# Chunked state recurrence and two feed-forward layers on one core: direct scores for eight tiles, causality by a product, weights decoded in the prologue, mixing by a shifted column, weights on 64-byte lines

## The chip, the core and the metric

The kernel runs on one core of a Trainium2 chip. The metric is device time in microseconds (us) for one execution; lower is better. The engines are TensorE (PE in the profile; PEld is its weight load), VectorE (DVE), ScalarE (ACT), GpSimd (POOL) and SyncE (SP), which here only issues transfers. TensorE's products read SBUF and write PSUM.

## The reference, cut to what matters

```python
def _attn_ref(x, a, B, C):                       # batch 4, heads 8, S 768, D 32, N 16, chunk 32
    cum = np.cumsum(la, axis=-1)
    L = np.exp(cum[:, :, :, None] - cum[:, :, None, :]) * causal
    M = np.einsum('bhin,bhjn->bhij', Cc, Bc) * L
    y_intra = np.einsum('bhij,bhjd->bhid', M, xc)
    y_inter = np.einsum('bhin,bhnd->bhid', Cc, state) * np.exp(cum)[:, :, :, None]
    state = decay_full * state + sum_j(Bc x xc * decay_from_j)
...
def _moe_ref(x, mu_k, mu_r, w_k, w_v, w_r):      # batch 4, S 768, d 256, d_ff 1024
    xk = mu_k * x + (1.0 - mu_k) * x_prev        # x_prev: the token before, 0 at a batch's start
    xr = mu_r * x + (1.0 - mu_r) * x_prev
    k = np.maximum(xk @ w_k, 0.0)
    v = k * k @ w_v
    return sigmoid(xr @ w_r) * v
...
def _moe2_ref(x, w_in, w_out):                   # 3072 tokens, d 256, d_ff 2048
    h = x @ w_in
    return (h - np.tanh(h)) @ w_out
```

## The kernel before

The recurrence is computed in 24 tiles of 128 tokens (six in each of four batches). For a tile, `decays` multiplies prepared rows into differences of summed logarithms (`pd`), ScalarE takes their exponential into `L`, GpSimd's `causal` clears what lies in the future, `scores` makes C times B for 8 heads (`pcb`), VectorE's `mask` multiplies the two in place, and `outputs` multiplies `L` with x and adds the carried state (`py`); `next_state` and `tile_out` write the state and the result `xall` (256 channels on 2 x 128 partitions, tokens along the free dimension).

`scores` has two forms. Tiles 0 to 3 are direct: B as it lies in memory (16 states of 8 heads on 128 partitions) is the stationary operand, and the moving one is `cm`, C spread to one block of columns for each head with zeros elsewhere, which `head_columns` builds on VectorE and GpSimd; both are plain float32. Tiles 4 to 23 take B and C in high and low parts from `st`: `bc_load` loads, `bc_high` (ScalarE) and `bc_low` (VectorE) split, `bc_write` stores them to memory, and `bc_read` loads them in another order, for two tiles at a time.

The first feed-forward layer works on six blocks of 512 tokens. `shift` takes the difference of a block with itself one token later, `mix` makes xk and xr from it, `high` and `low` split them for exact products; `up`, `relu`, `square`, `high`, `low`, `down_part` follow four times per block, and `receptance` and `sigmoid` give the gate. The second layer has six blocks of eight units (`up2`, a polynomial for the tanh, `down2`): 12 products of 512 columns up and 12 down in each. All of its products are three for one (high x high, low x high, high x low).

Weights are decoded on the chip: `decode` fetches a chunk of 8-byte numbers (`raw`, two buffers), squares a part on ScalarE, and takes `top`, `sign`, `bottom`, `guard` on VectorE, `high` on either and `low` on VectorE. The first layer has nine such chunks, the second sixteen; the second layer's live where the recurrence's tiles lay, and are decoded when these are done with.

The order is written in two ways. START lists the prologue by hand: the setup of the decay rows, tiles 0 and 1 and their loads. Everything after it is tasks that `Plan.run` places one by one on the engines by its own costs, with ranks (RANK_T, RANK_F and the like) to choose between ready ones; what comes out is a fixed order for each engine. Where such an order puts an instruction behind one that waits, it waits too.

In each partition the first layer's weights begin at a multiple of 64 bytes, and the second layer's, which are laid out from the memory's other end, 32 bytes past one.

Of the kernel before, what the change touches and what calls it, by code (L numbers as in the profile page):

```python
# [9 lines left out]
F32R = mybir.dt.float32r  # L10
U32 = mybir.dt.uint32
# [5 lines left out]
P = 128  # L17
# [7 lines left out]
BLK = 512  # L25
# [3 lines left out]
NP2 = DFF2 // (2 * P)  # L29
NU2 = NBLK * NP2  # L30
# [4 lines left out]
RANK_F0, RANK_F, RANK_R, RANK_U, RANK_D = 30.0, 27.0, 9.0, 5.5, 16.1  # L35
RANK_G0, RANK_G, RANK_LAG = 173.3, 1.4, 9.7
RANK_W0, RANK_W = 0, 5.5
RANK_X0, RANK_X = 105.0, 5.2
# [12 lines left out]
    Da Dc neg idle za kr1 kr0 cA seg Dla Db lA hA Da2 hm cC warm Dca rA cB rh lB rl Db2 cD g2 lC zb Dx lD kr2 g1 Dc2 Dc1 W  # L51
    hB Dnr g0 tri Dx2 rB las d0 r2 bd p00 d1 heads dec p01 Dnk m0 p10 p11 w1 w0 m1 ps g4 o0 nu W gs cum o1 g3 k1 z1
# [130 lines left out]
def chain_kernel(ctx, tc, xb, a, an, a0, bt, bc, mu_k, mu_r, w_k, w_v, w_r, w_in, w_out, out):  # L183
# [25 lines left out]
    def vec(tag, dtype=F32, n=BLK):  # L209
# [3 lines left out]
    nuk = const.tile([P, 2], F32, name="nuk")  # L213
    nur = const.tile([P, 2], F32, name="nur")
# [3 lines left out]
    carry = const.tile([P, 2, NBLK], F32, name="carry")  # L218
    sums = const.tile([P, NU2 + 1], F32, name="sums")
    ones = const.tile([P, 1], F32, name="ones")  # L220
    okc = const.tile([P, 1], F32, name="okc")
# [4 lines left out]
    xall = zp.tile([P, 2, NTOK], F32, name="xall")  # L226
# [12 lines left out]
        pair=Ring(3), xb=Ring(2, 0, 1), bc=Ring(3, 0, 1, 2), hl=Ring(1), st=Ring(2, "c0", "c1"), L=Ring(2, 0, 1), bp=Ring(3, 0, 1), cp=Ring(2, 0),  # L239
        er=Ring(1, 0), erl=Ring(2, 0), state=Ring(2, 0, 1), raw=Ring(2, 0, 1), x=Ring(WORK["xh"], "b0"), l=Ring(WORK["l"], "p0"), h=Ring(WORK["h"], "p0", "p1"),  # L240
        s=Ring(WORK["s"], "p0"), acc=Ring(1), ob=Ring(3), raw2=Ring(2), f=Ring(WORK["f"], "p0", "p1"), wd=Ring(1), keep=Ring(2), wd2=Ring(1), keep2=Ring(2),
# [17 lines left out]
    def decode(n, job, pool, two, rank, after=(), fetched=False):  # L259

        N, ring = 2 * CW, R["raw" + two]
        raw = None if fetched else add(dict(S=0.42), lambda e: fetch(job()[0], n, pool()), after, rank, [(ring, n)], dma=1.35)
        use = [(ring, n)]

        def square(e):
# [3 lines left out]
        def top(e):  # L269
# [15 lines left out]
        def low(e):
# [3 lines left out]
        sq = add(dict(A=t_act(N)), square, [raw], rank, [keep], use)  # L289
        t1 = add(dict(V=t_dve2(N)), top, [raw], rank, [wd], use, port=True)  # L290
        t2 = add(dict(V=t_dve(N)), sign, [t1], rank, uses=use, port=True)
        t3 = add(dict(V=t_dve(N)), bottom, [t2], rank, uses=use, port=True)
        t4 = add(dict(V=t_dve(N)), guard, [t3, sq], rank, (), [wd, keep], port=True)
        t5 = add(dict(A=t_act(N), V=t_dve2(N)), high, [t4], rank, (), [keep], port=True)
        t6 = add(dict(V=t_dve(N)), low, [t5], rank, (), [keep], port=True)
        return t6, t6
# [41 lines left out]
    def bc_load(k):  # L338
        nc.sync.dma_start(out=bc_tile(k), in_=bc[:, :, k * GT:(k + 1) * GT])
# [726 lines left out]
```

## Time and profile before

| | |
|---|---|
| time, median of 3 runs | 542.42 us (541.08 to 545.35) |
| the profiled execution's own time | 544.08 us |
| its span, first to last instruction | 542.4 us |
| PE busy | 506.3 us, 93% |
| DVE busy | 425.1 us, 78% |
| ACT busy | 311.0 us, 57% |
| POOL busy | 43.4 us, 8% |
| mean granted TensorE clock | 0.954 |

A busy share is an average over stages with different limits: the recurrence's first tiles, a stretch in which tiles and the first layer alternate, the rest of the first layer beside the decoding of the second's weights, and the second layer by itself. A matmul's end is modelled and matmuls overlap, so the beat of a dense stretch is read from the starts of its rows.

### The profile page before, as it was taken

To read this page: it belongs to the slowest core of one execution; us is meant where nothing else is said; L and a number is where in the kernel's file an instruction comes from. 1 tells how busy PE (TensorE), PEld (TensorE's weight loads), DVE (VectorE), ACT (ScalarE), POOL (GpSimd) and SP (SyncE) were. 2 spreads that over 40 slices of the span, in tenths; PEclk is the share of its full clock that TensorE was granted. 3 is DMA by queue.
4 is the path that set the end of the run, shared out by engine and by line. 5 is a ranking of instruction groups with operands and counts; after the bars stand their busy time and mean duration, and the time that the engine had idled before them with its cause. 6 is when DMAs were issued, how large, how long until landed. Compare 5 with 4: busy or idle time off the path is not lost.

```text
span 542.4 us, 7272 instructions
## 1 busy us (share of the span) xinstructions
PE 506.3 (93%) x2754; PEld 384.8 (71%) x2754; DVE 425.1 (78%) x548; ACT 311.0 (57%) x394; POOL 43.4 (8%) x49
## 2 busy tenths in 40 slices
PE   5857779999999999999999999999999999999994
PEld 2424457777677778878768878887887887888783
DVE  8779889886875989999999977756867667775671
ACT  3334356567575567766665566456665566546650
POOL 8312100111211200000000000000000000000000
PEclk9775589999999999999999999999999999999999
DMA  4489996978765033232300000001001001000101
GB/s 130 136 217 244 227 253 158 195 180 174 151 118 99 1 118 116 79 95 102 114 1 1 0 17 24 1 0 40 0 1 40 0 2 39 1 0 1 39 2 44
DMA packets 27015, 42.82 MB, mean 79 GB/s; under 512 B 2766, under 2 KB 16390, under 8 KB 26974
## 3 DMA queue, kind: packets, MB, share of 16 engines
q1 hardware_dynamic: 26974, 42.29, 31.0%
q8 instruction: 24, 0.39, 0.3%
q14 instruction: 17, 0.14, 0.1%
HBM read 33.67 MB, written 8.59 MB: 78 GB/s over the span
## 4 chain that ended last, share of the span: by engine, by line
PE 76%; DVE 12%; DMA 7%; issue 2%; ACT 2%; SPq 1%; POOL 0%; POOLq 0%; ACTq 0%; DVEq 0%
PE acc L743 11%; PE acc L745 11%; PE acc L744 11%; PE ph L733 8%; PE ph L736 8%; PE ph L734 8%; PE pk L733 4%; PE pk L734 3%; PE pk L736 3%; PE py L492 2%; DMA st<-dbc 2%; PE pd L407 2%; PE pcb L457 2%; DMA raw<-in_w_k 1%; DVE wd L274 1%
## 5 line engine op out<-in xcount | busy, mean ns | idle before, releaser
L874 DVE SCALAR_TENSOR_TENSOR f<-f,s 128x1024 f32<-128x1024 f32 (+1 forms) x49 | 58.9, 1202 | 64.9 <-ACT f L870 64.3
L869 ACT ACTIVATE s<-ph 128x1024 f32<-128x1024 f32 (+1 forms) x49 | 49.3, 1006 | 88.7 <-PE ph L736 88.1
L745 PE MATMUL acc<-l,wouth 128*128 128x512 f32 x192 | 76.0, 396 | 1.1 <-DVE l L887 1.1
L743 PE MATMUL acc<-h,wouth 128*128 128x512 f32 x192 | 76.3, 397 | 0.8 <-DVE flag L945 0.8
L733 PE MATMUL ph<-xh,winh 128*128 128x512 f32 x192 | 76.0, 396 | 0.0
L744 PE MATMUL acc<-h,woutl 128*128 128x512 f32 x192 | 75.8, 395 | 0.0
L734 PE MATMUL ph<-xh,winl 128*128 128x512 f32 x192 | 75.7, 394 | 0.0
L300 ACT ACTIVATE h<-f 128x1024 fp32r<-128x1024 f32 (+1 forms) x54 | 56.3, 1043 | 15.1 <-PE acc L744 8.0
L878 DVE TENSOR_TENSOR f<-ph,f 128x1024 f32<-128x1024 f32 (+1 forms) x49 | 58.8, 1200 | 3.5
L736 PE MATMUL ph<-xl,winh 128*128 128x512 f32 x192 | 60.4, 395 | 0.0
L887 DVE TENSOR_TENSOR l<-f,h 128x1024 fp32r<-128x1024 f32 (+1 forms) x49 | 58.5, 1195 | 0.5
L870 ACT ACTIVATE f<-s,pbias 128x1024 f32<-128x1024 f32 (+1 forms) x49 | 55.6, 1135 | 1.6
L743 PEld LDWEIGHTS acc<-h,wouth 128*128 128x128 f32 x192 | 36.0, 187 | 10.8 <-ACT ob L300 1.1
L745 PEld LDWEIGHTS acc<-l,wouth 128*128 128x128 f32 x192 | 36.0, 187 | 10.6 <-DVE l L887 1.9
L306 POOL TENSOR_SCALAR_AFFINE_SELECT L<-L 128x1024 f32<-128x1024 f32 (+1 forms) x26 | 31.2, 1204 | 142.7 <-ACT L L412 133.2
L736 PEld LDWEIGHTS ph<-xl,winh 128*128 128x128 f32 x192 | 35.9, 187 | 9.1 <-DVE xl L857 0.4
L733 PEld LDWEIGHTS ph<-xh,winh 128*128 128x128 f32 x192 | 36.0, 187 | 8.9
L734 PEld LDWEIGHTS ph<-xh,winl 128*128 128x128 f32 x192 | 36.0, 187 | 8.7
L744 PEld LDWEIGHTS acc<-h,woutl 128*128 128x128 f32 x192 | 36.0, 188 | 8.5
L733 PE MATMUL pk<-xh,wkh 128*128 128x512 f32 x96 | 40.6, 422 | 0.0
L734 PE MATMUL pk<-xh,wkl 128*128 128x512 f32 x96 | 39.0, 406 | 0.0
L743 PE MATMUL acc<-h,wvh 128*128 128x512 f32 x96 | 38.3, 399 | 0.1
(142 smaller groups left out, 848.0 us busy)
## 6 DMA issues: line engine op xcount, KB each, us to landing
dbc<-hl SPq DMA_DIRECT2D x20, 256.0 KB
st<-dbc SPq DMA_DIRECT2D x20, 256.0 KB
st<-dbc SPq DMA_DIRECT2D x40, 128.0 KB
xbt<-in_xb SPq DMA_DIRECT2D x12, 384.0 KB
bct<-in_bc SPq DMA_DIRECT2D x11, 384.0 KB
raw<-in_w_in SPq DMA_DIRECT2D x8, 512.0 KB
raw<-in_w_out SPq DMA_DIRECT2D x8, 512.0 KB
out<-ob SPq DMA_DIRECT2D x12, 256.0 KB
```

Source lines behind the costliest of these rows:

```text
L300: A.activation(out=out, in_=in_, func=AF.Copy)
L733: PE.matmul(o, wh[:, k, ms], hi[:, k], start=k == 0, stop=False)
L734: PE.matmul(o, wl[:, k, ms], hi[:, k], start=False, stop=False)
L736: PE.matmul(o, wh[:, k, ms], lo[:, k], start=False, stop=k == 1)
L743: PE.matmul(acc[:, c], wh[:, k, cs], h[:, e], start=first, stop=False, skip_group_check=True)
L744: PE.matmul(acc[:, c], wl[:, k, cs], h[:, e], start=False, stop=False, skip_group_check=True)
L745: PE.matmul(acc[:, c], wh[:, k, cs], l[:, e], start=False, stop=last, skip_group_check=True)
L869: A.activation(out=s, in_=phs[j, i][:, e], func=AF.Square, accum_out=sums[:, c:c + 1])
L870: A.activation(out=qs[j, i][:, e], in_=s, func=AF.Square, scale=PA, bias=pbias)
L874: V.scalar_tensor_tensor(out=q, in0=q, scalar=PG, in1=s, op0=ALU.add, op1=ALU.mult)
L878: V.tensor_tensor(out=q, in0=phs[j, i][:, e], in1=q, op=ALU.mult)
L887: V.tensor_tensor(out=l[:, e], in0=qs[j, i][:, e], in1=f(h[:, e]), op=ALU.subtract)
```

## The change

Eight tiles in place of four are direct. C is laid out with its zeros on the host (`c4`, one 128 x 512 block of float32 per tile) and loaded; `head_columns` goes. The blocks are arranged so that the two halves of a tile use 64 partitions each. The split, store and reload are left out for those eight tiles, of whose `bc` only the third part is loaded. In those tiles causality is no longer cleared by GpSimd: a second product adds -32768 above the diagonal to `pd` before the exponential. The rows of `kr` for the first batch come from `kl` instead of the copy in memory. The prologue decodes the first two weight chunks step by step, the order of the nine chunks is another, and the three `kr` copies move to ScalarE. `xall` gets a zero column ahead of each batch, so that the previous token is the column before: `shift` and its carried columns go, `mix` becomes a scaled copy on ScalarE and one operation on VectorE (`mix_ahead`). One 32-byte tile (`okc`) moves into the second layer's pool, which puts that layer's weights at multiples of 64 bytes. Some ranks change.

```diff
+ND = 8
+NW = 2
...
-RANK_F0, RANK_F, RANK_R, RANK_U, RANK_D = 30.0, 27.0, 9.0, 5.5, 16.1
-RANK_G0, RANK_G, RANK_LAG = 173.3, 1.4, 9.7
-RANK_W0, RANK_W = 0, 5.5
-RANK_X0, RANK_X = 105.0, 5.2
+RANK_F0, RANK_F, RANK_R, RANK_U, RANK_D = 30.0, 27.0, 9.0, 5.5, 16.07
+RANK_G0, RANK_G, RANK_LAG = 144.89, 0, 6.52
+RANK_W0, RANK_W = 1.49, 5.5
+RANK_X0, RANK_X = 105.0, 6.14
...
-    xall = zp.tile([P, 2, NTOK], F32, name="xall")
+    xall = zp.tile([P, 2, NTOK + 8], F32, name="xall")
...
     def bc_load(k):
-        nc.sync.dma_start(out=bc_tile(k), in_=bc[:, :, k * GT:(k + 1) * GT])
+        w = slice(0, 3) if 2 * k >= ND else slice(2, 3)
+        nc.sync.dma_start(out=bc_tile(k)[:, w], in_=bc[:, w, k * GT:(k + 1) * GT])
...
     def rows(i):
...
+        if b:
+            nc.sync.dma_start(out=f(krs[i % 3][ONE:ONE + 2]), in_=dcum[:, b, :, ts])
+            return
+        for x, o in enumerate((CH, CL)):
+            nc.sync.dma_start(out=f(krs[i % 3][ONE + x:ONE + x + 1]), in_=f(kls[0][o:o + NH, ts]))
...
-            PE.matmul(pd[:, g], kls[b % 2][:, t * P:(t + 1) * P], krs[i % 3][:, 4 * g:4 * g + 4], start=True, stop=True)
+            PE.matmul(pd[:, g], kls[b % 2][:, t * P:(t + 1) * P], krs[i % 3][:, 4 * g:4 * g + 4], start=True, stop=i >= ND)
+            if i < ND:
+
+                PE.matmul(pd[:, g], ident, after.unsqueeze(1).to_broadcast([P, NH // 2, P]), start=False, stop=True)
...
-            if split:
-                causal(i, g)
...
-    def direct(i, pcb, g):
-        PE.matmul(pcb[:, 2 * g:2 * g + 2], bs[0][:, i * P:(i + 1) * P], cm[i][:, 4 * g:4 * g + 4], start=True, stop=True)
+    def c4_load(lo, hi):
+        o = cms[lo // NQ].rearrange("p a q s -> p (a q s)").rearrange("p (t c) -> p t c", c=BLK)
+        nc.sync.dma_start(out=o[:, lo % NQ:lo % NQ + hi - lo], in_=c4[lo:hi].rearrange("t p c -> p t c"))
+
+    def direct(i, pcb):
+        for g in range(2):
+            r = slice(64 * g, 64 * g + 64)
+            PE.matmul(pcb[:, g], bs[0][r, i * P:(i + 1) * P], cm[i][r], start=True, stop=True)
...
-            return lambda: V.tensor_copy(krs[i], neg.unsqueeze(2).to_broadcast([NR, NH, P]))
+            return lambda: A.activation(out=krs[i], in_=neg.unsqueeze(2).to_broadcast([NR, NH, P]), func=AF.Copy)
...
-            SEL[i] = put(dict(G=1.17), lambda e, i=i: causal(i), [E[i]], at(i) - 0.9, (), [(R["L"], i)])
+            SEL[i] = E[i] if i < ND else put(dict(G=1.17), lambda e, i=i: causal(i), [E[i]], at(i) - 0.9, (), [(R["L"], i)])
...
-    def shift(j):
...
-        V.tensor_tensor(out=u[:, :, 1:], in0=xall[:, :, t0 + 1:t1], in1=xall[:, :, t0:t1 - 1], op=ALU.subtract)
...
     def mix(nm, j):
         full = mixes[nm, j] = vec("f")
-        nu = nuk if nm == "k" else nur
+        x, o = block(j, 1), halves(full)
         for c in range(2):
-            V.scalar_tensor_tensor(out=full[:, c], in0=us[j][:, c], scalar=nu[:, c:c + 1], in1=xall[:, c, j * BLK:(j + 1) * BLK], op0=ALU.mult, op1=ALU.add)
+            A.activation(out=o[:, c], in_=x[:, c], func=AF.Copy, scale=mus[nm][:, c:c + 1])
+
+    def mix_ahead(nm, j):
+        x, o = block(j, 0), halves(mixes[nm, j])
+        for c in range(2):
+            V.scalar_tensor_tensor(out=o[:, c], in0=x[:, c], scalar=oms[nm][:, c:c + 1], in1=o[:, c], op0=ALU.mult, op1=ALU.add)
...
-        jobs1 = [jk[0], jr[0], jk[1], jk[2], jv[0], jk[3], jv[1], jv[2], jv[3]]
+        jobs1 = [jk[0], jk[1], jv[0], jk[2], jr[0], jv[1], jk[3], jv[2], jv[3]]
...
+            w2["okc"] = w2p.tile([P, 1], F32, name="okc")
             w2["ob"] = w2p
```

On VectorE, before, this is what stood between the mask of tile 1 and the mask of tile 2 (`L<-pcb,L` is a mask, `wd` and `keep` belong to a weight chunk, `bp` to `weigh`, `hl` to `bc_low`, `cm` is C spread by head); the rows shown begin at the last spreading of C.

```order
L435 TENSOR_TENSOR cm<-bct,hm 128x1024
L271 TENSOR_SCALAR wd<-raw 128x512
L422 TENSOR_TENSOR bp<-xbt,dec 128x128
L274 SCALAR_TENSOR_TENSOR wd<-raw,wd 128x512
L347 TENSOR_TENSOR hl<-bct,hl 128x2x256
L277 SCALAR_TENSOR_TENSOR wd<-raw,wd 128x512
L422 TENSOR_TENSOR bp<-xbt,dec 128x128
L280 SCALAR_TENSOR_TENSOR keep<-keep,wd 128x512
L422 TENSOR_TENSOR bp<-xbt,dec 128x128
L271 TENSOR_SCALAR wd<-raw 128x512
```

The first chunk's decoding began only after tile 1 and the spreading of C, with the split of B and C in its midst.

The same place on VectorE now, up to the masks of tiles 2 and 3.

```order
L640 TENSOR_SCALAR omr<-mur 128x2
L289 SCALAR_TENSOR_TENSOR wd<-raw,wd 128x512
L292 SCALAR_TENSOR_TENSOR wd<-raw,wd 128x512
L295 SCALAR_TENSOR_TENSOR keep<-keep,wd 128x512
L301 TENSOR_TENSOR wkl<-keep,wkh 128x2x256
L451 TENSOR_TENSOR bp<-xbt,dec 128x128 x2
L426 COPY erl<-er 128x4
L404 TENSOR_TENSOR cp<-bct,er 128x256 x2
L451 TENSOR_TENSOR bp<-xbt,dec 128x128
L493 TENSOR_TENSOR L<-pcb,L 128x1024 x2
L286 TENSOR_SCALAR wd<-raw 128x512
```

Both of the first two chunks are now finished ahead of the masks of tiles 2 and 3, the two masks stand together, and no row spreads or splits C.

On TensorE, before, these rows led from tile 4 to the first product of the first layer (`pk`); `pcb<-st` are scores from the reloaded parts.

```order
L407 MATMUL pd<-kr,kl_98 128x512 x2
L457 MATMUL pcb<-st 128x128 x16
L481 MATMUL py<-xbt,bp 32x64 x4
L486 MATMUL py<-cp,ns 64x128 x4
L492 MATMUL py<-L,xbt 32x128 x8
L407 MATMUL pd<-kr,kl_99 128x512 x2
L486 MATMUL py<-cp,ns 64x128 x4
L492 MATMUL py<-L,xbt 32x128 x8
L407 MATMUL pd<-kr,kl_99 128x512 x2
L457 MATMUL pcb<-st 128x128 x16
L733 MATMUL pk<-xh,wkh 128x512
```

Two groups of scores that wait for a reload stood ahead of the first layer's first product.

On TensorE now, the rows up to that product.

```order
L468 MATMUL pcb<-cm,h 128x512 x2
L420 MATMUL pc<-kl_101,heads 128x512
L420 MATMUL pc<-kl_101,heads 128x256
L435 MATMUL pd<-kr,kl_101 128x512
L438 LDWEIGHTS ident
L438 MATMUL pd<-after,ident 128x512
L435 MATMUL pd<-kr,kl_101 128x512
L438 LDWEIGHTS ident
L438 MATMUL pd<-after,ident 128x512
L512 MATMUL py<-cp,ns 64x128 x4
L518 MATMUL py<-L,xbt 32x128 x8
L468 MATMUL pcb<-cm,h 128x512 x2
```

The first layer still begins behind tile 5's outputs and tile 6's scores, but these scores no longer use the reload, and each `pd` has two more products. From tile 8 on, the number of first-layer products that stand ahead of each tile's outputs is almost that of before: 60 ahead of tile 8 and 336 ahead of tile 23 in both orders.

## Rows read from the trace of the kernel before

**Rows 1.** The page, 40 slices of 13.56 us: TensorE's granted clock, DMA busy.

```profile
PEclk9775589999999999999999999999999999999999
DMA  4489996978765033232300000001001001000101
```

**Rows 2.** Busy time by stage; columns: PE, PEld, DVE, ACT, POOL, clock, DMA share, GB/s.

```profile
0.00:60.60 60.60, 38.34 (x253) 19.52 (x255) 51.19 (x99) 23.56 (x38) 23.01 (x33) 0.71 0.73 185
60.60:87.70 27.10, 23.22 (x137) 16.89 (x136) 23.39 (x37) 13.72 (x19) 1.09 (x1) 0.77 0.94 224
87.70:191.00 103.30, 102.33 (x891) 74.55 (x894) 83.48 (x124) 64.78 (x75) 19.34 (x15) 1.00 0.62 132
191.00:292.00 101.00, 99.14 (x441) 79.57 (x442) 97.28 (x136) 69.79 (x86) 0.00 (x0) 1.00 0.26 84
300.00:520.00 220.00, 220.00 (x944) 176.18 (x943) 154.30 (x136) 129.80 (x163) 0.00 (x0) 1.00 0.03 13
```

**Rows 3.** The chain that ended last, 16 to 90 us: start, length, what.

```profile
36.01 9.14 DMA st<-dbc
...
56.16 7.65 DMA raw<-in_w_k
```

**Rows 4.** VectorE in order of time: start, length, line, operation, tiles [idle before].

```profile
19.64 1.22 DVE L467 TENSOR_TENSOR L<-pcb,L 128x1024 f32<-128x1024 f32 x1 [0.59 <-PE pcb L441]
...
35.70 0.69 DVE L286 TENSOR_TENSOR wrl<-keep,wrh 128x512 fp32r<-128x512 f32 x1 [0.70 <-ACT wrh L300]
...
46.08 1.58 DVE L274 SCALAR_TENSOR_TENSOR wd<-raw,wd 128x512 uint32<-128x512 uint32 x1
...
60.59 1.21 DVE L771 TENSOR_TENSOR xl<-f,xh 128x1024 fp32r<-128x1024 f32 x1
...
65.31 0.68 DVE L274 SCALAR_TENSOR_TENSOR wd<-raw,wd 128x512 uint32<-128x512 uint32 x1
```

**Rows 5.** VectorE's groups by shape: busy us, mean ns.

```profile
L752 DVE TENSOR_TENSOR s<-xall 128x1022 f32<-128x1022 f32 x6 | 7.3, 1215 | 0.0
...
L347 DVE TENSOR_TENSOR hl<-bct,hl 128x512 fp32r<-128x512 f32 x10 | 6.8, 682 | 0.0
...
L632 DVE CAST kr<-neg 66x1024 fp32r<-66x1024 f32 x3 | 2.2, 768 | 0.5 <-POOL neg L306 0.5
...
L435 DVE TENSOR_TENSOR cm<-bct,hm 128x1024 f32<-128x1024 f32 x1 | 1.2, 1214 | 0.0
```

**Rows 6.** ScalarE's groups by shape.

```profile
L343 ACT ACTIVATE hl<-bct 128x512 fp32r<-128x512 f32 x10 | 6.3, 628 | 14.1 <-DMA dbc<-hl 12.1 <-DMA bct<-in_bc 1.9
...
L412 ACT ACT_TABLE_LOAD x4 | 5.1, 1283 | 0.1
```

**Rows 7.** TensorE in order of time, recurrence.

```profile
15.08 4.45 PE L441 MATMUL pcb<-cm,xl 128*128 128x512 f32 x6
...
29.70 1.96 PE L441 MATMUL pcb<-cm,xl 128*128 128x512 f32 x4 [0.61 <-ACT L L412]
...
48.31 0.44 PE L481 MATMUL py<-xbt,bp 128*32 128x64 f32 x8
...
49.31 1.08 PE L492 MATMUL py<-L,xbt 128*32 128x128 f32 x16
50.32 1.22 PE L407 MATMUL pd<-kr,kl 66*128 66x512 f32 x2
...
59.76 1.94 PE L457 MATMUL pcb<-st 64*128 64x128 f32 x15 [2.23 <-DMA st<-dbc]
```

**Rows 8.** TensorE in order of time, dense: first layer (201), second layer (310).

```profile
201.14 0.39 PE L733 MATMUL pk<-xh,wkh 128*128 128x512 f32 x1
...
203.86 0.39 PE L733 MATMUL pk<-xh,wkh 128*128 128x512 f32 x1
...
310.58 0.40 PE L743 MATMUL acc<-h,wouth 128*128 128x512 f32 x1
...
313.38 0.40 PE L743 MATMUL acc<-h,wouth 128*128 128x512 f32 x1
```

More of the change, by code (lines that the diff above doesn't have):

```diff
@@ L10 @@
 F32R = mybir.dt.float32r
+BF16 = mybir.dt.bfloat16
 U32 = mybir.dt.uint32
@@ L257, in fetch, with decoding, square, top @@
         nc.sync.dma_start(out=raws[n], in_=src)
[L259 to L265, printed above, removed]
+    def decoding(n, job, pool):
+        def square():
             keeps[n] = pool().tile([P, 2, CW], F32, tag="keep", bufs=2, name="keep")
             A.activation(out=keeps[n], in_=f(raws[n][..., 1]), func=AF.Square)
-        def top(e):
+        def top():
@@ L291, in decode @@
-        t2 = add(dict(V=t_dve(N)), sign, [t1], rank, uses=use, port=True)
-        t3 = add(dict(V=t_dve(N)), bottom, [t2], rank, uses=use, port=True)
-        t4 = add(dict(V=t_dve(N)), guard, [t3, sq], rank, (), [wd, keep], port=True)
+        return square, top, sign, bottom, guard, high, low
+    def decode(n, job, pool, two, rank, after=()):
+        N, ring = 2 * CW, R["raw" + two]
+        square, top, sign, bottom, guard, high, low = decoding(n, job, pool)
+        raw = add(dict(S=0.42), lambda e: fetch(job()[0], n, pool()), after, rank, [(ring, n)], dma=1.35)
+        use = [(ring, n)]
+        wd, keep = (R["wd" + two], n), (R["keep" + two], n)
+        sq = add(dict(A=t_act(N)), lambda e: square(), [raw], rank, [keep], use)
+        t1 = add(dict(V=t_dve2(N)), lambda e: top(), [raw], rank, [wd], use, port=True)
+        t2 = add(dict(V=t_dve(N)), lambda e: sign(), [t1], rank, uses=use, port=True)
+        t3 = add(dict(V=t_dve(N)), lambda e: bottom(), [t2], rank, uses=use, port=True)
+        t4 = add(dict(V=t_dve(N)), lambda e: guard(), [t3, sq], rank, (), [wd, keep], port=True)
@@ L459, in mask @@
     def mask(i, split=False):
-        m, pcb = mt[i].rearrange("p c h i -> p (c h) i"), pcbs.pop(i)
-        if i >= 4:
-            m = m.rearrange("p (q g) i -> p g q i", g=2)
+        m, pcb = mt[i], pcbs.pop(i)
+        if i >= ND:
+            m = m.rearrange("p c h i -> p (c h) i").rearrange("p (q g) i -> p g q i", g=2)
             V.tensor_tensor(out=m, in0=pcb, in1=m, op=ALU.mult)
             return
-        c = pcb.rearrange("p q g i -> p (q g) i")
-        for h in [slice(0, 4), slice(4, 8)] if split else [slice(0, 8)]:
-            V.tensor_tensor(out=m[:, h], in0=c[:, h], in1=m[:, h], op=ALU.mult)
+        m = m.rearrange("p c h i -> p c (h i)")
+        for g in [slice(0, 1), slice(1, 2)] if split else [slice(0, 2)]:
+            V.tensor_tensor(out=m[:, g], in0=pcb[:, g], in1=m[:, g], op=ALU.mult)
     pys = {}
@@ L585, in first_rows @@
             return fn
-        def third_rows():
-            for x, o in enumerate((CH, CL)):
-                nc.sync.dma_start(out=f(krt[ONE + x:ONE + x + 1, :, 2]), in_=f(kls[0][o:o + NH, GT:GT + P]))
         def t_cum():
@@ L652, in prologue @@
         )
+        for n, steps in enumerate(parse):
+            fns.update(zip((x + str(n) for x in ("sq", "tp", "sg", "bt", "gd", "hi", "lo")), steps))
         for o in START:
@@ L706, in attention @@
                 BPt[i] = put(dict(V=t_dve(P)), lambda e, i=i: weigh(i), [XL.get(k)], at(i) - 1.0, [(R["bp"], i)], [(R["xb"], k)], port=True)
-            SC[i] = put(dict(P=0.3 if i > 3 else 1.86), lambda e, i=i: scores(i), [BR.get(k)], at(i) - 0.5, [(R["pair"], ("pcb", i))])
-            if i < 4:
-                R["x"].use("b0", SC[i])
-                R["st"].use("c1", SC[i])
+            SC[i] = put(dict(P=0.3 if i >= ND else 1.2), lambda e, i=i: scores(i), [BR.get(k)], at(i) - 0.5, [(R["pair"], ("pcb", i))])
+            if i < ND:
+                R["h"].use("b0", SC[i])
+                R["st"].use(i // NQ, SC[i])
             else:
@@ L1036, in parity, with apart @@
         return states(v).reshape(NQ, 2, NS, NTOK).transpose(1, 2, 0, 3).reshape(P, NTOK)
+    def apart(v):
+        r = np.zeros((ND, 2, NQ, NS, NQ, P), v.dtype)
+        t = states(v)[:, :ND * P].reshape(2, NQ, NS, ND, P)
+        for q in range(NQ):
+            r[:, :, q, :, q] = t[:, q].transpose(2, 0, 1, 3)
+        return r.reshape(ND, P, NQ * P)
     def columns(v):
```

178 lines of the change are left out of this document (78 added, 100 removed).

## The prediction

> **What bounds the kernel now.** I read the page's slices first, then the busy times by stage, the chain of waits, and VectorE's and TensorE's rows in order of time. The slices give the clock: TensorE is granted less than full speed from the second slice to the sixth (13.6 to 81 us), half of it in the fourth and fifth, and the DMA engines are at 0.9 from the fourth to the sixth [rows 1]. The stages [rows 2] show five different limits. The second layer by itself (300 to 520) has 220.00 us of PE in 220. From 87.7 to 191 PE has 102.33 of 103.3 and VectorE 83.48. From 191 to 292, where the second layer's weights are decoded, PE has 99.14 of 101 and VectorE 97.28: both are full. The first 60.6 us are another thing: PE 38.34, VectorE 51.19, ScalarE 23.56, no engine full, VectorE nearest to it. The end of this stage is the low half `xl` of the first block at 60.59 on VectorE [rows 4], and the first product of the first layer follows at once, so whatever shortens VectorE's queue up to `xl`, waits included, starts the dense work earlier. The chain of waits there goes through reloads of `st` (9.14) and weight chunks `raw` (7.65) [rows 3]: VectorE's queue has instructions that wait for these.
>
> The base is the profiled execution, 544.08 us, which is 1.7 above the median of the runs, 542.42. The sum is made against 544.1, and 1.7 is taken off at the end.
>
> **A. From the start to tile 8's outputs: −13.** First VectorE's queue up to `xl`, 51.19 busy of 60.6, 9.4 idle [rows 2]. These rows leave it: three `kr` copies, 2.2; the spreading of C, 1.2 and a half-size one at 0.6; two `hl` splits at 0.68; the shift of the first block, 1.22 and its little column rows, together 1.4 [rows 5]. Three decode steps at 0.68 and less now come after `xl`, about 1.7. Together 8.5. Second, rows that last longer than the same row elsewhere: `sign` took 1.58 at 46.08 while POOL cleared a tile, and 0.68 at 65.31, when it did not [rows 4]. Eight rows before `xl` are stretched like that, by 6.7 in all. POOL's clearing of tiles 0 to 7 goes, and its share of spreading C; its setup of masks stays, for which I keep 0.7. So 6.0 more go and 51.2 − 8.5 − 6.0 = 36.7 stay busy.
>
> What waits then? Up to tile 1's mask, at 19.64 before [rows 4], the queue waits for the decay rows, a chain through all engines that the change shortens little: ScalarE gets the `kr` copies (on VectorE 0.77 each [rows 5]) and with them an early change of its table (1.28 [rows 6]), while a stretched cast on VectorE of like size goes. I put the mask at 18 and the idle time to there at 8. The two chunks decoded step by step go to ScalarE and back, 0.7 each, as before the low part at 35.70 [rows 4]. Tiles 3 to 5 may wait for TensorE, 2.5: its clock is low there, and a tile's rows cost, cold, 1.22 for `pd`, 1.00 from the first part of `py` to its last and 1.08 for that [rows 7], the two causality products 0.9 at half the beat of the dense 512-column products [rows 8], and the scores. These I halve: a direct tile's four records, 1.96 warm and about 3 cold [rows 7], become two pairs on 64 partitions each. That such a pair runs side by side no row for the float32 form shows; the nearest are the reloaded scores, 15 records on 64 partitions in 1.94 [rows 7], whose starts come in pairs. Side by side a tile's scores cost 0.98 warm and 1.5 cold, one after the other twice that. The first gives 1.22 + 2.08 + 0.9 + 1.5 = 5.7 a tile, so 23 us for tiles 2 to 5, which fits into the 30 between mask 1 and `xl`; the second gives 29 and ends that cover. Idle time: 8 + 1.4 + 2.5 = 12 less a little, say 11. So `xl` stands at 36.7 + 11 = 48 in place of 60.6: −12.6.
>
> From there to tile 8's outputs took 27.1 [rows 2]: 60 dense products, which are 13.6 at full speed [rows 8], three tiles at some 2.3, and half speed for part of it. The same 60 products stand there now. Tiles 6 and 7 have two more products for causality each, 0.46 warm, and scores at 0.98 instead of half of 1.94; no tile waits for a reload. That is a gain of 1 at most, and I take −0.4. Together −13.
>
> The transfers: `c4` adds 2 MB, B 0.4, and 1 MB of `bc` goes; two writes and reloads (3 MB) go, but these are later. At 185 GB/s for a share of 0.73 [rows 2], 2.4 MB are 9.5 us of all 16 engines. The first two slices, 27 us, are 0.4 busy [rows 1] and have 16 free. So I cost them at nothing; the cover is gone if the blocks of `c4` stand in SyncE's queue ahead of what tiles 0 and 1 need, or if `raw` comes later by them.
>
> Bounds of A: if everything that VectorE loses shows and its waits don't grow, `xl` is at 46 and the clock is up sooner, −18. If tiles 2 to 5 wait for TensorE (6 us) and the loads cost a little, −6.
>
> **B. Tile 8 to tile 23: 0, within 2.** PE-bound, so the shifts that leave VectorE are covered. ScalarE gets four scaled copies of 512 columns per block, 0.63 each like its `hl` rows [rows 6], and has 64.78 busy of 103.3 [rows 2]. TensorE's rows there keep their number.
>
> **C. 191 to 292: −1.5.** Three shifts at 1.22 [rows 5], 3.7 with their small rows, leave a full VectorE, but PE has at most 1.9 of idle time to give back [rows 2]. Bounds −4 (the modelled ends of products hide idle time) and +3 (the chunks of the second layer come in another rhythm, and a late one stops its first products).
>
> **D. The second layer's beat: −7.5.** In the first layer at 201, 12 products take 2.72 us from start to start, 226.7 ns each; in the second, 12 take 2.80, 233.3 each [rows 8]. Same shapes, same engine, full clock. VectorE is nearly full in the faster stretch and 70% busy in the slower [rows 2], so it isn't the neighbour. What differs is the place of the stationary operand: 64-byte multiples in the first layer, 32 bytes past in the second. 6 x 8 x 24 = 1152 products by 6.7 ns are 7.7; a little goes since products after a break run at 230 and more also in the first layer. Bounds 0 and −7.7.
>
> Against it stands a rule. In the Trainium skill, "SBUF — State Buffer", section "Specifications (TRN2)", memory has lines of 16 bytes, and only a step to another line costs. A shift by 32 bytes leaves such lines whole, so by that rule alone the beat would stay at 233 and the sum would lack its 7.5. That is rival 1; the trace shows two beats with place as the one difference that I find, but no row shows one operand at both places.
>
> **The sum.** −13 + 0 − 1.5 − 7.5 = −22; 544.1 − 22 = 522.1, and 1.7 less is 520.5. Its own range is 516 to 526.
>
> **Rivals.**
> 1. The place of the weights isn't the cause of the slow beat: −14.5 remain, 528. For it: two layers differ in much else (the order of loads, PSUM tiles). Against: the beat is one value within each. Chance 0.14.
> 2. The first stage stays with its transfers: the 9.5 us of added loads are not covered, since the DMA engines are full from the fourth slice on [rows 1] and the chain went through `raw` already [rows 3]. Then A shrinks from 13 to 4: 529.5. For it: those rows. Against: 3 MB of the split's and reload's transfers leave the same stretch. Chance 0.15.
> 3. More is won: A is 18 and C 4, for which VectorE need only lose what I listed and TensorE be up in clock earlier: 512 to 513. Against: the chain of the decay rows. Chance 0.12.
> 4. Slower than before, by the clock. TensorE's clock fell and stayed low in the first stage, when it was idle for a third of the time [rows 1, 2]. It now has less to do there. If the 1.2 GHz level stays on through the dense work, 1 us of that work takes 2; before, the clock was at 0.8 in the slice in which the dense work got going (67.8 to 81.4) and above 0.9 in the next [rows 1]. It takes 22 us of dense work more at 1.2 GHz to undo the gain; with 28 it is 548. Against: once the dense products stand close together, from the seventh slice on, the clock is never low again. Chance 0.03.
>
> **How the numbers follow.** The forecast has 0.54, and what I have not thought of 0.02. The likeliest case gives 520.5. The range takes in rivals 1, 2 and most of 3's side, with A's bounds: 507 to 533, which leaves out rival 4 and the far ends. A change under 1%, 5.4 us, can't be told from none, so faster means under 537.0: rivals 1 to 3 and the forecast nearly whole, 0.92; between the two 0.05, by A and D both at their weak ends; slower 0.03.
>
> **What would show it.** A: `xl` of the first block near 48, tile 8's outputs near 74, and no stretched rows beside POOL between tile 1 and tile 8. D: 12 products of the second layer in 2.72. C: the second layer begins some 14 us earlier. If `xl` comes at 55 or later, look at its waits: for `raw` or `c4` (rival 2), or for TensorE at its low level. The forecast is wrong if the beat stays, if the list of waits of VectorE grows by as much as its work shrinks, or if a late chunk of the second layer's weights stops TensorE around 260.

## The result and the profile after

The changed kernel took 526.38 us (median of 4 runs, 524.56 to 528.8) against 543.0 for the kernel before in the same comparison: ratio 0.9712, 95% interval 0.9655 to 0.9769. That is 16.6 us less by the medians, in the forecast's direction and range (507 to 533), with 520.5 forecast. Its profiled execution took 526.32, with a span of 524.6 where before had 542.4: 17.8 less. The profile of before lay 1.1 above the median of this comparison and that of after at its own, so the pair of profiles shows more than the runs.

The page's clock and DMA lines, to be laid beside [rows 1]:

```profile
PEclk8775999999999999999999999999999999999998
DMA  4768888887850222233200010001001001000101
```

A slice is 13.1 us here. The clock is up from the fifth slice on (52 us), before from the seventh. The DMA engines are at 0.6 to 0.8 from the second slice to the eleventh; before, they were at 0.4 in the first two.

The busy time by stage, cut at the places that answer to those of [rows 2] (PE, PEld, DVE, ACT, POOL, clock, DMA share, GB/s):

```profile
0.00:48.50 48.50, 36.26 (x223) 14.80 (x223) 35.02 (x83) 26.21 (x41) 5.64 (x22) 0.74 0.71 217
48.50:72.00 23.50, 22.29 (x154) 13.75 (x154) 20.64 (x34) 15.58 (x22) 1.79 (x1) 0.88 0.83 197
72.00:175.00 103.00, 101.85 (x879) 74.02 (x878) 84.99 (x123) 67.36 (x80) 18.90 (x15) 1.00 0.64 138
180.00:280.00 100.00, 97.65 (x426) 79.28 (x425) 97.85 (x135) 72.58 (x89) 0.00 (x0) 1.00 0.26 84
285.00:505.00 220.00, 220.00 (x962) 180.49 (x962) 159.14 (x140) 138.73 (x172) 0.00 (x0) 1.00 0.03 13
```

The first stage is where the time went: VectorE 35.0 busy where it had 51.2, POOL 5.6 where it had 23.0, and 48.5 us in place of 60.6. The stretch from tile 8 to tile 23 (72 to 175) is as long as before. The next one is still full on VectorE, 97.85 of 100. In the second layer the same 220 us hold 962 recorded products where they held 944.

VectorE's rows in order of time: a `sign` step of a weight chunk, the low half of the first block, the masks of tile 8 and of tile 23.

```profile
45.80 0.69 DVE L289 SCALAR_TENSOR_TENSOR wd<-raw,wd 128x512 uint32<-128x512 uint32 x1
...
48.53 1.22 DVE L782 TENSOR_TENSOR xl<-f,xh 128x1024 fp32r<-128x1024 f32 x1
...
72.02 1.21 DVE L489 TENSOR_TENSOR L<-pcb,L 128x1024 f32<-128x1024 f32 x1
...
175.04 1.22 DVE L489 TENSOR_TENSOR L<-pcb,L 128x1024 f32<-128x1024 f32 x1
```

The low half stands at 48.53, 12.1 earlier than in [rows 4]; the step that took 1.58 beside POOL takes 0.69. The masks of tiles 8 and 23 in the trace of before:

```profile
85.59 1.22 DVE L463 TENSOR_TENSOR L<-pcb,L 128x1024 f32<-128x1024 f32 x1
...
188.36 1.22 DVE L463 TENSOR_TENSOR L<-pcb,L 128x1024 f32<-128x1024 f32 x1
```

The gain is 13.6 at the one and 13.3 at the other.

TensorE's rows of the second layer, twelve products apart, to be laid beside [rows 8]; then the direct scores of a tile, at the low and at the full clock, beside [rows 7]:

```profile
31.67 2.01 PE L468 MATMUL pcb<-cm,h 64*128 64x512 f32 x4
...
34.82 1.13 PE L468 MATMUL pcb<-cm,h 64*128 64x512 f32 x4
...
322.36 0.39 PE L759 MATMUL acc<-h,wouth 128*128 128x512 f32 x1
...
325.11 0.39 PE L759 MATMUL acc<-h,wouth 128*128 128x512 f32 x1
```

Twelve products take 2.75 us, 229 ns each: neither the 233.3 of before nor the first layer's 226.7. A tile's four score records take 1.13 where a tile's four took 1.96, so the two halves do run side by side (the records of a pair start 6 to 8 ns apart).

The second layer's first product starts at 245.43 (before 259.56, 14.1 earlier). Behind it TensorE stops four times, and each stop waits for VectorE's queue or for ScalarE behind it; before, there was one such stop, the last row here, and one of 0.65 in the first layer at 236.86.

```profile
258.63 0.50 PE L759 MATMUL acc<-h,wouth 128*128 128x512 f32 x1 [0.72 <-ACT h L322]
...
259.89 0.51 PE L761 MATMUL acc<-l,wouth 128*128 128x512 f32 x1 [0.52 <-DVE l L896]
...
266.09 0.50 PE L749 MATMUL ph<-xh,winh 128*128 128x512 f32 x1 [0.87 <-DVE f L887]
...
268.44 0.51 PE L761 MATMUL acc<-l,wouth 128*128 128x512 f32 x1 [0.24 <-DVE l L896]
```

```profile
274.31 0.50 PE L745 MATMUL acc<-l,wouth 128*128 128x512 f32 x1 [1.09 <-DVE l L887]
```

So the accounts of the pair of profiles are: start to tile 8 −13.6; tile 8 to tile 23 +0.2; from there to the second layer's first product −0.8; the rest, −3.7, is the beat (1152 products by 4.3 ns are −5.0) and the stops (+1.3).

One pair of profiles is a small sample. Experiments 1 to 5 below leave all orders as they are and change only places in memory, so with them there are two profiles with the order of before and five with that of the changed kernel. Their means give −11.9 for the first part (tile 8's mask at 82.8 and 85.6 before, at 70.4 to 73.6 now), +1.3 for the second and −0.9 for the third. With −3.7 for the rest that is −15.2, near the 15.6 of the ratio.

### The profile page after: what moved, and what is told of

It reads as the page before. It is cut to its first block, busy times and chain, and to the rows that moved or that the text cites. A ratio compares the mean times of both kernels' runs of the same rounds, so it can differ in the third digit from the quotient of the medians.

```text
span 524.6 us, 7223 instructions
## 1 busy us (share of the span) xinstructions
PE 500.3 (95%) x2754; PEld 379.5 (72%) x2754; DVE 411.0 (78%) x530; ACT 328.1 (63%) x413; POOL 26.3 (5%) x38
## 4 chain that ended last, share of the span: by engine, by line
PE 66%; DVE 21%; DMA 6%; ACT 2%; issue 2%; SPq 1%; DVEq 0%; ACTq 0%
PE acc L759 10%; PE acc L761 10%; PE acc L760 10%; PE ph L750 8%; PE ph L752 8%; PE ph L749 8%; DVE l L782 3%; DVE wd L289 2%; DVE keep L295 2%; DVE wd L292 2%; PE py L518 2%; PE pk L749 2%; DMA h<-in_bt 2%; PE pd L435 2%; PE pk L750 1%
## 5 line engine op out<-in xcount | busy, mean ns | idle before, releaser
L322 ACT ACTIVATE h<-f 128x1024 fp32r<-128x1024 f32 (+1 forms) x62 | 64.7, 1046 | 35.9 <-PE acc L760 29.1
L761 PE MATMUL acc<-l,wouth 128*128 128x512 f32 x192 | 74.8, 389 | 0.8 <-DVE l L896 0.8
L761 PE MATMUL acc<-l,wvh 128*128 128x512 f32 x96 | 37.6, 391 | 0.3 <-DVE l L782 0.3
L750 PE MATMUL pk<-xh,wkl 128*128 128x512 f32 x96 | 37.8, 394 | 0.0
```

What stands on the lines that cost most here:

```text
L322: A.activation(out=out, in_=in_, func=AF.Copy)
L750: PE.matmul(o, wl[:, k, ms], hi[:, k], start=False, stop=False)
L761: PE.matmul(acc[:, c], wh[:, k, cs], l[:, e], start=False, stop=last, skip_group_check=True)
```

## The experiments

Theories: **queue**, that VectorE's queue up to the first block sets the start, so that what leaves it is the gain there; **place**, that where the stationary operand starts sets the dense beat. Rivals: the start is set by transfers and reloads, or by TensorE's low clock; the beat belongs to the layer or to the order of the work. Ratios are to the kernel before in the same comparison; the changed kernel's is 0.9712 (0.9655 to 0.9769). Where an experiment's interval overlaps that one, as in most of them, the times alone don't part the two, and the rows are what is read.

**1. The weights' place alone, in the kernel before.**

```diff
+            w2["ob"], w2["okc"] = w2p, w2p.tile([P, 1], F32, name="okc2")
-            w2["ob"] = w2p
```

> The kernel before, with only the second layer's four weight tiles moved down by 32 bytes per partition (the last reduction's 32-byte result is laid beside them), so that they start 64 bytes past a multiple of 128 as in the changed kernel; the first layer's weights, all work tiles and every engine's order stay. Theory place: the start of the stationary operand sets the beat; the second layer goes from 233.3 to 229 ns per product, the first stays at 226.7, the time falls by 1152 x 4.3 ns = 5 us (ratio 0.991). Rival order: the beat comes from the order of the work or from what else runs; it stays at 233.3 and the time stays (within 1 us). The forecast's own size of the term: 226.7 ns and -7.5 us.

Ratio 0.9926 (0.9898 to 0.9953), some 4 us. TensorE, second layer:

```profile
323.62 0.39 PE L743 MATMUL acc<-h,wouth 128*128 128x512 f32 x1
...
326.37 0.39 PE L743 MATMUL acc<-h,wouth 128*128 128x512 f32 x1
```

2.75 for twelve products: 229, as in the changed kernel. Place holds, order falls, and the forecast's 7.5 us is too much.

**2. The place undone in the changed kernel.**

```diff
+    ones, okc = const.tile([P, 1], F32, name="ones"), const.tile([P, 128], F32, name="okc")[:, 0:1]
...
-            w2["okc"] = w2p.tile([P, 1], F32, name="okc")
+            w2["okc"] = okc
```

> The changed kernel with the second layer's weights back where they were before (96 bytes past a multiple of 128); the tile that had pushed them stands in the left part of the memory with its length rounded so that all else keeps its place within 512 bytes. Theory place: the second layer's beat is 233.3 ns again, the time rises by 5 us (ratio to the changed kernel 1.009, about 531). Rival order: it stays at 229 and 526.

Ratio 0.9799 (0.9759 to 0.9839), 532.6 us. The rows:

```profile
322.52 0.39 PE L759 MATMUL acc<-h,wouth 128*128 128x512 f32 x1
...
325.32 0.39 PE L759 MATMUL acc<-h,wouth 128*128 128x512 f32 x1
```

2.80 for twelve, 233.3 again, and the time rises by 0.0087 of 542, 4.7 us. Both ways the place alone moves the beat.

**3. A multiple of 128 bytes.**

```diff
-            w2["okc"] = w2p.tile([P, 1], F32, name="okc")
+            w2["okc"] = w2p.tile([P, 24], F32, name="okc")[:, 0:1]
```

> The changed kernel with the second layer's weights 64 bytes further down, at a multiple of 128 bytes, as the first layer's are. Theory place, with steps of 128 bytes: the beat is that of the first layer, 226.7 ns, and the time falls by 1152 x 2.3 ns = 2.6 us (about 523.7). Rival 64: multiples of 64 bytes are all alike and 229 has another cause in the second layer; the beat stays at 229 and the time at 526. All orders stay.

Both were wrong: ratio 0.978 (0.974 to 0.9821), 530.1 us, some 4 us more than the changed kernel.

```profile
322.92 0.40 PE L759 MATMUL acc<-h,wouth 128*128 128x512 f32 x1
...
325.70 0.40 PE L759 MATMUL acc<-h,wouth 128*128 128x512 f32 x1
```

2.78 to 2.79 for twelve; over the whole layer the mean is 232.4 ns. A rounder address is not a better one. What had stayed alike in the first layer was that its weights start at a multiple of 512 bytes, as its moving operands do.

**4. A multiple of 512 bytes.**

```diff
-            w2["okc"] = w2p.tile([P, 1], F32, name="okc")
+            w2["okc"] = w2p.tile([P, 120], F32, name="okc")[:, 0:1]
```

> The changed kernel with the second layer's weights at a multiple of 512 bytes, where the first layer's weights and the moving operands of both layers already are. All orders stay. So far the beat was 226.7 ns with weights at 0 of 512, 229.0 at 448, 232.4 at 384 and 233.3 at 480. Theory place by 512: the beat is 226.7 ns as in the first layer, the time falls by 1152 x 2.3 = 2.6 us against the changed kernel (about 524). Rival layer: 226.7 belongs to the first layer for another reason (its moving tiles, its PSUM tiles); the beat is 229 or more, the time 526 or more.

```profile
322.92 0.39 PE L759 MATMUL acc<-h,wouth 128*128 128x512 f32 x1
...
325.64 0.39 PE L759 MATMUL acc<-h,wouth 128*128 128x512 f32 x1
```

2.72 for twelve: 226.7 ns, the first layer's beat, over the whole second layer. Ratio 0.9675 (0.9652 to 0.9697), 524.35 us: the fastest of the versions that leave nothing out. The beat, worth 2.6 us, parts it from the changed kernel; the times don't.

**5. The moving operands pushed by 32 bytes, the weights at 0 of 512**, on top of experiment 4.

```diff
-    ones = const.tile([P, 1], F32, name="ones")
+    ones, okc = const.tile([P, 1], F32, name="ones"), const.tile([P, 1], F32, name="okc")
```

> As the run before it, but all that lies in the left part of the memory (moving operands of both layers, first layer's weights) starts 32 bytes past a multiple of 512; the second layer's weights stay at 0 of 512. Theory distance: what counts is the distance of stationary and moving operand; the first layer (distance 0) keeps 226.7 ns, the second (distance 480, as in the kernel before) has 233.3. Theory weights alone: the second layer, with its weights at 0, has 226.7, and the first, at 32, something else, 229 or more.

The first layer (192.38 to 195.10) and the second (322.66 to 325.46):

```profile
192.38 0.39 PE L759 MATMUL acc<-h,wvh 128*128 128x512 f32 x1
...
195.10 0.39 PE L759 MATMUL acc<-h,wvh 128*128 128x512 f32 x1
...
322.66 0.39 PE L759 MATMUL acc<-h,wouth 128*128 128x512 f32 x1
...
325.46 0.39 PE L759 MATMUL acc<-h,wouth 128*128 128x512 f32 x1
```

The first layer, with weights and moving operands both 32 past, keeps 2.72; the second, with its weights at the very place that gave 226.7 in experiment 4, has 2.80. So it isn't the weights' place but their distance from the moving operand's: 0 of 512 gives 226.7, 448 gives 229.0, 384 gives 232.4, 480 gives 233.3. The one run took 532.9 us and is read for its beats alone. It moved all that lies on that side of the memory, tiles of other engines too; that it is TensorE's own moving operand that counts is the plain reading and was not tried by itself.

**6. GpSimd's clearing back in tiles 0 to 7.**

```diff
+            if i < ND:
+                causal(i, g)
-                PE.matmul(pd[:, g], ident, after.unsqueeze(1).to_broadcast([P, NH // 2, P]), start=False, stop=True)
```

> The changed kernel with GpSimd clearing the future in tiles 0 to 7 again after the exponential, in place of the second product; all engines' other work in the same order. Theory sharing: VectorE's rows beside GpSimd's clearing are stretched (0.68 to 1.58 us) and the mask waits for the clearing, 1.2 us a tile; the first block's low half goes from 48.5 to 52 to 55 us and the time rises by 3 to 6 us. Rival TensorE: the two products saved, 0.9 to 1.3 us a tile at the low clock, bring as much as the stretching costs; the low half stays within 1.5 us and the time within 2 us.

Ratio 0.9739 (0.9698 to 0.9779), 529.6 us. VectorE's rows: a mask that waits for the clearing, the stretched step, the low half.

```profile
41.62 1.23 DVE L492 TENSOR_TENSOR L<-pcb,L 128x1024 f32<-128x1024 f32 x1 [0.99 <-POOL L L328]
...
47.02 1.58 DVE L289 SCALAR_TENSOR_TENSOR wd<-raw,wd 128x512 uint32<-128x512 uint32 x1
...
50.26 1.21 DVE L781 TENSOR_TENSOR xl<-f,xh 128x1024 fp32r<-128x1024 f32 x1
```

The mechanism is there, stretch and wait, but the low half moves by 1.7 only, under the 3.5 to 6.5 expected; the five profiles of one order differ by 1.9 there (46.84 to 48.79). The time moved by 1.5 (by the ratios) to 3.2 us (by the medians).

**7. No causality in tiles 0 to 7.**

```diff
-                PE.matmul(pd[:, g], ident, after.unsqueeze(1).to_broadcast([P, NH // 2, P]), start=False, stop=True)
...
-            A.activation(out=m[:, g].rearrange("p g h i -> p g (h i)"), in_=pd[:, g], func=AF.Exp)
+            A.activation(out=m[:, g].rearrange("p g h i -> p g (h i)"), in_=pd[:, g], func=AF.Exp, scale=0.0 if i < ND else 1.0)
```

> The changed kernel with the causality of tiles 0 to 7 left out altogether (neither product nor clearing; their exponential is taken with scale 0 so that it stays finite, which leaves out the decay as well). Orders stay. Prices the second product. Theory covered: 0.65 us twice a tile at the low clock lie beside VectorE's queue up to the first block and on the path only after it; the low half stays at 48.5 within 1 us, the time falls by at most 1.5 us. Rival TensorE: in the first stage TensorE's low clock sets the masks of tiles 2 to 5; the low half comes 2 to 4 us earlier, the time falls by 3 us or more.

Ratio 0.9752 (0.9695 to 0.9808), 527.6 us. The low half:

```profile
47.86 1.22 DVE L779 TENSOR_TENSOR xl<-f,xh 128x1024 fp32r<-128x1024 f32 x1
```

No gain. The second product is covered, at 0.65 a piece at the low clock and 0.39 at the full one in the changed kernel's rows.

**8. Half of C left out of the loads.**

```diff
-    cm = [cms[i // NQ].rearrange("p a q s -> p (a q s)")[:, i % NQ * BLK:(i % NQ + 1) * BLK] for i in range(ND)]
+    cm = [cms[i // NQ].rearrange("p a q s -> p (a q s)")[:, i % NQ * BLK:(i % NQ + 1) * BLK] for i in [*range(NQ), *range(NQ)]]
...
-            De3=lambda: c4_load(4, 8)
+            De3=lambda: None
```

> The changed kernel without the load of the C blocks of tiles 4 to 7 (1 MB), which then use those of tiles 0 to 3: their scores are left out of the result. Orders stay but for that one transfer. Theory covered: these bytes lie where the DMA engines have room; the first block's low half stays at 48.5 within 1 us and the time within 1.5 us. Rival transfers: 1 MB at 250 KB per us is 4 us by which weight chunks and x come earlier; the low half comes 2 to 4 us earlier, and the time falls by as much.

Ratio 0.9718 (0.97 to 0.9735): the time didn't move. The low half:

```profile
47.19 1.22 DVE L782 TENSOR_TENSOR xl<-f,xh 128x1024 fp32r<-128x1024 f32 x1
```

In its profile tile 8's mask came at 68.5, which is 1.9 ahead of the earliest of the other runs with this order, so in single executions something may be won; the median shows none of it. The added loads are covered to within some 2 us.

**9. No decoding in the prologue**; its fourteen steps (`sq0` to `lo1`) leave START.

```diff
-NW = 2
+NW = 0
...
-        raw = add(dict(S=0.42)
+        raw = None if n < 2 else add(dict(S=0.42)
```

> The changed kernel without the decoding of the first two weight chunks in the hand-written prologue: the planner places all nine, as in the kernel before; their two first loads stay where they are. Theory queue: VectorE's work up to the first block's low half is the same, only its order changes, and that queue sets the start; the low half stays at 48.5 within 1.5 us, the time within 2 us of 526. Rival early decode: the gain of the first stage comes from decoding while the queue waits for the decay rows; the low half comes 4 us later or more and the time rises to 530.

Ratio 0.9763 (0.9748 to 0.9778), 528.7 us. Low half:

```profile
50.87 1.22 DVE L782 TENSOR_TENSOR xl<-f,xh 128x1024 fp32r<-128x1024 f32 x1
```

Between the two: 2.3 later, 2.8 us slower by the ratios. Early decoding fills waits of VectorE's queue and is worth 2.3 of the 12.1 by which the low half came earlier. Behind the low half the planner's order is another one: tile 8's mask stands at 72.01, where it stood, and tile 23's comes 3.5 later.

**10. The shift's VectorE work put back.**

```diff
+        if nm == "k":
+            for c in range(2):
+                V.tensor_tensor(out=x[:, c], in0=x[:, c], in1=x[:, c], op=ALU.max)
```

> The changed kernel with VectorE work of the shift's size put back: per block two operations of 512 columns that take the block's maximum with itself (1.4 us; the result is unchanged) ahead of the mixing for xk; order otherwise the same. Prices the shift that the change removed, six times 1.4 us. Theory by stage: one in the first stage shows (1.4), two in the PE-bound stretch don't, the last three, where VectorE is full, show in part; together 1.5 to 4 us. Rival hidden: VectorE's removal is worth nothing outside the first block, 1.5 us or less. Rival queue: all show, 8 us.

528.8 us, ratio 0.9793 (0.9733 to 0.9852): 2.4 us more by the medians, 4.4 by the ratios. By stage: low half at 49.41, +0.9; tile 23's mask at 175.44, +0.4; the second layer's first product at 248.31, +2.9. The work of the middle blocks vanishes, and that of the last two, in the stretch where VectorE is full, shows nearly whole: 2.5 of 2.6 (two blocks at 1.29). The stretch from tile 23's mask to the second layer's first product took 70.4 in all five profiles of the changed kernel's order and takes 72.9 here. "By stage" holds, but only two blocks fall there, not three.

**11. TensorE kept busy in the first stage**, on top of experiment 4.

```diff
+        for _ in range(8 if 0 < i < ND else 0):
+            PE.matmul(py[:, 1, 2 * P:4 * P], ident, after.unsqueeze(1).to_broadcast([P, 2, P]), start=True, stop=True, skip_group_check=True)
```

> The changed kernel with the second layer's weights at a multiple of 512 bytes, and TensorE kept busy in the first stage: in tiles 1 to 7 eight products of 256 columns whose result nobody reads stand just ahead of the outputs that wait for the mask. Without them this version took 524.4 us (ratio 0.9675). Theory clock: the granted clock falls in the first stage because TensorE waits there; with the gaps filled it stays higher up to the first layer, tiles 2 to 8 go faster, and the time falls by 2 to 5 us. Rival length: the added products (0.8 us a tile at full speed, 1.7 at half) end later than the masks and delay the outputs; the clock stays as it is and the time rises by 1 to 5 us.

The added products share a bank with the outputs and clear part of them, so this is a run for its time alone. From 31 to 49.2 us the granted clock was 0.93; in the profile of experiment 4, from 31 to 48.8, it was 0.69. The time was 522.7, ratio 0.9684 (0.9639 to 0.973), against 0.9675 without: the clock can be held up, and that this pays is not shown. The low half, at 49.25, didn't come earlier, which speaks against the low clock as what sets the start.

**12. Four direct tiles in place of eight.**

```diff
-ND = 8
+ND = 4
...
-RANK_G0, RANK_G, RANK_LAG = 144.89, 0, 6.52
+RANK_G0, RANK_G, RANK_LAG = 144.89, 0.01, 6.52
...
-            De3=lambda: c4_load(4, 8)
+            De3=lambda: None
```

> The changed kernel with four direct tiles in place of eight: tiles 4 to 7 take split, stored and reloaded parts and GpSimd's clearing, as before the change; a rank of the second layer is 0.01 in place of 0, without which no order came out. Theory queue: VectorE gets two splits (0.68 each) and rows stretched by four clearings (some 3 us), and the masks of tiles 4 to 7 wait for reloads; the first block's low half comes at 52 to 56 in place of 48.5 and the time rises by 4 to 7 us. Rival: the gain of the first stage is in the decoding, the kr copies and tiles 0 to 3 alone; the low half stays at 49 to 50 and the time within 2 us.

Ratio 1.0004 (0.9972 to 1.0035): 542.1 us, all of the gain gone, far beyond what either theory gave. TensorE's longest wait between 30 and 100 us (in total, times, longest), and three of its four pieces:

```profile
PE pcb L483 <- DMA st<-dbc: 9.0, 4, 6.3
```

```profile
44.49 0.44 PE L483 MATMUL pcb<-st 64*128 64x128 f32 x1 [6.30 <-DMA st<-dbc]
...
46.03 1.94 PE L483 MATMUL pcb<-st 64*128 64x128 f32 x15 [1.10 <-DMA st<-dbc]
...
73.63 1.94 PE L483 MATMUL pcb<-st 64*128 64x128 f32 x15 [1.40 <-DMA st<-dbc]
```

VectorE's low half and the masks of tiles 8 and 9 (with four direct tiles the rows of L489 begin with tile 4, so tile 8's is the fifth of them):

```profile
51.59 1.22 DVE L782 TENSOR_TENSOR xl<-f,xh 128x1024 fp32r<-128x1024 f32 x1
...
75.16 1.21 DVE L489 TENSOR_TENSOR L<-pcb,L 128x1024 f32<-128x1024 f32 x1
...
83.34 1.22 DVE L489 TENSOR_TENSOR L<-pcb,L 128x1024 f32<-128x1024 f32 x1
```

The stage from the low half to tile 8's mask, and two stretches around and behind it:

```profile
51.60:75.16 23.56, 20.28 (x159) 14.54 (x160) 22.07 (x34) 15.20 (x21) 4.86 (x4) 0.86 1.01 235
70.00:80.00 10.00, 7.93 (x32) 6.20 (x32) 8.67 (x15) 3.52 (x6) 1.19 (x1) 0.66 1.05 247
90.00:100.00 10.00, 7.94 (x34) 5.79 (x32) 10.00 (x11) 6.40 (x8) 2.26 (x2) 0.68 0.85 200
```

The low half comes 3.1 later than in the changed kernel, with about the same VectorE work ahead of it (36.5 us), and tile 8's mask 3.1 later too. TensorE waits 7.4 us for `st` ahead of the low half and 1.6 behind it; the stage from there to tile 8's mask takes 23.6, as in the changed kernel (23.5), though the DMA engines are full (share 1.01). So 10.4 of the 13.6 us are still there at tile 8, less some 2 us of first-layer work (42 of its products are recorded ahead of that mask, 50 in the changed kernel). The rest of the gain goes later: tile 23's mask at 188.71 is 13.7 later, the second layer's first product at 255.90 is 10.5 later, and what follows takes 4.8 more. The granted clock falls again, to 0.66 and 0.68 in the two stretches shown, where the changed kernel has 1.00 from 60 us on. The reservation: the planner made another order out of this, with ranks set for eight tiles, and how much of the later loss is order and how much reloads isn't told apart. As a price of the reloads the run can be read up to tile 8 and no further.

## Why the prediction was right, and where it was off

**A, the start (−13 forecast, −13.6 in the pair of profiles, −11.9 over the seven).** The places came out as forecast: low half at 48.53 for 48, VectorE's busy time up to it 35.0 for 36.7 and idle 13.5 for 11, tile 8's mask 13.6 earlier. Some of this is luck: the misses in busy and idle time offset each other, and single profiles of one order lie some 3 us apart at tile 8. Side by side was the right choice for the scores (1.13 and 2.01 for forecast 0.98 and 1.5), the causality product is covered (experiment 7), and so are the loads to within some 2 us (experiment 8), so rival 2 fell. That the low clock sets the start, experiment 11 speaks against.

The reason given, VectorE's queue with its waits, is borne out piece by piece, not as a whole. What experiments 6, 9, 10 and 12 put back moves the low half by 1.7, 2.3, 0.9 and 3.1; that is at most 8.0 of 12.1, each known to 2 us or so, and 6 and 12 share part of their work. The `kr` copies and the spreading of C, which the sum also counted, were not put back by themselves. The sum had no term for reloads that hold up the queue ahead of the low half; experiment 12 prices them, two splits and four clearings together at 3.1. Behind the low half, "a gain of 1 at most" for the missing reloads holds: with the reloads of two pairs of tiles back, that stage is no longer than without.

**B (0).** As forecast: 103 us from tile 8's mask to tile 23's in the pair, as before; over the seven profiles 1.3 more, inside the 2 that were allowed.

**C (−1.5 forecast, +0.5 measured: −0.8 and the stops' +1.3).** The step counted three shifts in the stretch from 191 on. The trace of before has only the last of the six there, at 213.6. And there was less to win: from tile 23's mask to the second layer's first product, before and then after,

```profile
188.36:259.56 71.20, 70.48 (x329) 57.23 (x327) 67.85 (x100) 50.54 (x60) 0.00 (x0) 1.00 0.32 104
```

```profile
175.04:245.43 70.39, 70.39 (x330) 57.67 (x329) 66.00 (x94) 52.66 (x64) 0.00 (x0) 1.00 0.29 95
```

TensorE's idle time of 0.7 is gone, and no more was there. Part of VectorE's room was filled: ScalarE got the scaled copies, and the planner gave VectorE more of the work that either can do. VectorE's groups by shape, before (188.4 to 260.6) and then after (175 to 246.3), ReLU on `pk` and the square:

```profile
L790 DVE TENSOR_SCALAR f<-pk 128x1024 f32<-128x1024 f32 x1 | 1.2, 1214 | 0.0
```

```profile
L801 DVE TENSOR_SCALAR f<-pk 128x1024 f32<-128x1024 f32 x3 | 3.6, 1216 | 0.0
...
L808 DVE TENSOR_TENSOR f<-f 128x1024 f32<-128x1024 f32 x1 | 1.2, 1226 | 3.8 <-ACT f L799 3.8
```

These two groups are 3.6 us more, and ahead of the square VectorE waits 3.8 us for ScalarE. In all it is busy 2 us less than before, and eleven low parts of weight chunks come out of it in those windows where twelve did. That the decoding left over makes the four stops of the second layer's first units is likely, since they wait for VectorE or for ScalarE behind it; no run shows it by itself.

**D, the beat (−7.5 forecast, −5.0 measured).** The mechanism was right, rival 1 fell (experiments 1 and 2), and the size was off: "64-byte multiples" was read from two places, and the beat is set by the distance between the two operands. The change moved it from 480 to 448 of 512, which is worth 4.3 ns of the 6.6 that are to be had. The rule that was weighed, the 16-byte lines in the Trainium skill's "SBUF — State Buffer", section "Specifications (TRN2)", doesn't cover this: all the places tried are whole lines, and the beat differs by up to 3%. The Trainium skill, "TensorE: Matmul & The Clock Gate", section "Step-by-step: what each phase is for", says that loading the next weights takes no SBUF read bandwidth from the running product. A beat that a distance alone moves from 226.7 to 233.3 sits ill with that, but no run here shows that it is this load that collides, so the cause behind the distance stays open.

**The sum.** Of the 5.9 us between 520.5 and 526.4, C and D have 2.0 and 2.5, A and B give 0.3 back, and 1.7 is the step from the profile to the median, which I took off a sum whose changed kernel lies at its median. Rivals 3 and 4 didn't occur: the clock was up earlier than before.

## What to carry to other kernels

Where dense products stream through TensorE, put the stationary and the moving operands at the same place within 512 bytes, and read the beat from the starts of twelve products; a tile of a few bytes in a pool shifts all that comes behind it. When an engine's queue seems to set a stage, put its parts back one at a time and read where the stage's end moves, beside how far profiles of one order lie apart. A run for which the scheduler makes another order prices that order too: read it at the last place before the orders part, not by its time. Before counting on work that leaves a full engine, look up when its instructions really run, and what the scheduler may put in their place.

## What the runs showed of the hardware that was not expected

The beat of back-to-back 512-column products at the full clock took four values, by the distance of the operands' starts within 512 bytes: 226.7 ns at 0, 229.0 at 448, 232.4 at 384, 233.3 at 480. Moving both by 32 bytes changed nothing. Other distances, and whether 256 counts as 0, were not tried.

The first stage differs from run to run in one and the same order, and the granted clock with it. Page lines of the changed kernel are shown above (8775 in the first four slices); experiment 4, with the same order up to the second layer, has

```profile
PEclk9666889999999999999999999999999999999998
```

and its second layer begins at 249.27, while that of the changed kernel begins at 245.43. The two are 0.3 apart at the low half, 1.6 at tile 8's mask and 3.3 at tile 9's, so most of these 4 us arise between 49 and 86 us.
